# An attention, router and experts kernel: column-group logits for the last batch, held weight loads, choices as bits, four flag operations

## The chip, the cores and the metric

The kernel runs on one core of a Trainium2 chip, in one launch. The metric is the device time of that launch in microseconds. Five engines work at once and hand over by semaphores: TensorE (PE), VectorE (DVE), ScalarE (ACT), GpSimd (POOL) and SyncE (SP, which only issues DMA transfers here). Weight loads of TensorE are shown as PEld.

## What is computed

Windowed attention over 8 batches of 576 tokens with 8 heads of 64 gives a row x of 512 numbers for each of 4608 tokens. A router then assigns every token to one of 8 experts. It takes all 4608 x 8 logits from the largest down, and each expert takes at most 576 tokens. Each expert applies its two matrices to its tokens.

```python
# heads 0 to 3: the last 32 keys; heads 4 to 7: every 4th of the last 128
x = softmax(scale * q @ k.T, masked) @ v          # as 4608 rows of 512
logits = x @ w_gate                               # 4608 x 8
for idx in np.argsort(-logits.flatten()):
    tok, e = idx // 8, idx % 8
    if assigned[tok] >= 0 or counts[e] >= 576: continue
    assigned[tok] = e; counts[e] += 1
for e in range(8):
    mask = assigned == e
    out[mask] = np.maximum(x[mask] @ w1[e], 0) @ w2[e]
```

## The kernel before

The program lists its operations with the engine, a cost, what each depends on and a boost. A list scheduler (`Schedule`) in the program puts them in one order, and every engine executes its own in that order. So a changed cost or boost moves operations on all engines, even where the code beside it stays as it is. An engine stands still at an operation whose inputs are not there, and what is behind it on that engine waits too.

**Attention** runs batch by batch. `tokens()` (L652) computes the router's logits for the last batch alone (`DIRECT` = 7): in four groups, one for each 128 of the 512 features (`g`), it uses a tile of x as weights and 8 columns of the gate matrix as the moving side (L664). Copies (L674 on VectorE, L272 on ScalarE) bring the logits from PSUM to `Lt`, 36 chunks of 128 tokens with 8 logits. Earlier batches go another way: the gate matrix is the weights, in column groups (L597), and the logits come back through L605 and L618.

**The router** (class `Router`) works on `Lt`. `choose()` (L892) finds each token's best open expert (`M`), a sortable key and a one-hot row `oh0`. Where an expert has more than 576 candidates, a search over the keys finds its threshold. In the first round this is `search_alone()` (L835): coarse counts, then steps of flags and counts. VectorE writes the flags `G` for 36 chunks in `PARTS` = 5, 15 and 16 chunks of 16 columns (L792, L790), TensorE counts them with one matmul a chunk (L857), and VectorE and TensorE turn the counts into the next step's base (L870, L871). The later rounds' searches (`search`, `counts` L778) run beside the experts before them. `expert()` (L969) takes the largest full expert from `em`, and its index `eidx` (L976) is what SP reads to address the weights. `members()` marks its tokens (`pr` L983, `te` L985, `ge` L987); slots and a list `idx` of 576 tokens follow.

**The experts.** In each of 8 rounds `gather()` (L1242) fetches the 576 rows of x by five indirect DMAs on POOL (L1249, tiles `xg0` to `xg4`, from `xd` in DRAM), TensorE transposes them (L1263), ScalarE and VectorE split them into a high and a low part (`xh`, `xl`). GEMM1 is L1300, GEMM2 is L1342. `weights()` (L1140) loads `w1` and `w2` in 8 pieces each of 256 KB (`raw`, L1150, SP's queue), ScalarE makes the high part (`w1h`, `w2h`, L1137), and the low part comes from VectorE or, in the pairs of `ADDED`, from ScalarE and an accumulating DMA on POOL's queue (L1158, L1160). ScalarE also copies the output tiles `y` out of PSUM (L1137), and POOL scatters them (L1368). `behind()` (L1390) makes some loads of rounds 0 and 1 depend on the second gather:

```python
    def behind(r, f):
        return [got[r, 1]] if r < len(AHEAD_W) and f >= AHEAD_W[r] else []
```

Of the kernel before, what the change touches and what calls it, by code (L numbers as in the profile page):

```python
# [8 lines left out]
F32 = mybir.dt.float32  # L9
F32R = mybir.dt.float32r  # L10
BF = mybir.dt.bfloat16
I32 = mybir.dt.int32
U16 = mybir.dt.uint16
AF = mybir.ActivationFunctionType
OP = mybir.AluOpType
# [19 lines left out]
PARTS = (5, 15, 16)  # L35
# [4 lines left out]
RAW1, D_R, NQ, AHEAD_W = 8, 262, (2, 2), (3,)  # L40
# [19 lines left out]
def consts():  # L60
# [32 lines left out]
    f["pri"] = np.broadcast_to((NE - np.arange(NE))[None, :], (128, NE)).astype(np.float32)  # L93
# [149 lines left out]
def attention(tc, ctx, C, load_const, T, xd, Lt, R):  # L243
# [399 lines left out]
    def coarse(c0, c1, x, late):  # L643
        for c in range(c0, c1):
            g, used, use_ = PRE.take()
            f = op("DVE", 290, lambda c=c, g=g: R.coarse(c, g), [x, *used], late)
            counted[0] = op("PE", 60, lambda c=c, g=g: R.coarse_counts(c, g), [f, ready["c", 3], counted[0]], late)
            use_.append(counted[0])

    def tokens(un):  # L650

        b, u = un.b, un.u  # L652
        c0, c1 = b * S // 128, (b * S + S) // 128
        parts = [(c, 0, 128) for c in range(-(-b * S // 128), c1)]
        half = (c0, 64, 64) if b % 2 else (c1, 0, 64)
        late = B_K if b < B - 1 else B_E
        pt = Buf(PV)
        o = lambda c, p, n: pt.tile[p:p + n, NE * (c - c0):NE * (c - c0) + NE]

        def logits(gs):  # L660
            for c, p, n in parts + [half]:
                for g in gs:
                    t0 = 128 * c + p - b * S
                    nc.tensor.matmul(o(c, p, n), xt_[b, g // 2][0][:, g % 2, t0:t0 + n], wgp[:, g, :NE],  # L664
                                     start=(c == parts[0][0] and g == 0), stop=(g == 3), skip_group_check=True)

        t = un.op("PE", 1050, lambda: logits([0]), [*xt_[b][:3], ready["w"]], late, pt)
        t = un.op("PE", 1050, lambda: logits([1]), [t], late)
        t = un.op("PE", 1050, lambda: logits([2]), [t, *ch_[b]], late)
        t = un.op("PE", 1050, lambda: logits([3]), [t, *xt_[b]], late)  # L670
        for kk in range(2):
            xt_[b, kk][2].append(t)
        ca = parts[0][0]
        xs_ = [un.op("DVE", 200, lambda: nc.vector.tensor_copy(  # L674
            Lt[:, ca:c1], pt.tile[:, NE * (ca - c0):NE * (c1 - c0)].rearrange("p (c e) -> p c e", e=NE)), [t], late),
            un.op("ACT", 250, lambda: act(Lt[half[1]:half[1] + 64, half[0]], o(*half)), [t], late)]
        pt.users += xs_
        if b < B - 1:
            hl_.append(xs_[1])
        x = un.op("DVE", 1000, lambda: R.choose(c0, c1), [*xs_, *(hl_ if b == B - 1 else ())], late)  # L680
        coarse(c0, c1, x, B_P if b < B - 1 else late - u * P_U)
# [55 lines left out]
class Router:  # L737


    def __init__(self, tc, ctx, C, Lt):  # L740
        nc = tc.nc
        self.tc, self.C = tc, C
        self.pf = ctx.enter_context(tc.tile_pool(name="r_fix", bufs=1))
        self.Lt = Lt
        self.A = self.pf.tile([128, NCH], F32, name="A")
        self.PR = self.pf.tile([128, 32], F32, name="PR")
        self.M = self.pf.tile([128, NCH], F32, name="M")
        self.V0 = self.pf.tile([128, NCH], F32, name="V0")
# [148 lines left out]

    def copies(self, oh, eng):
# [70 lines left out]
    def expert(self, em):  # L969

        nc, pw = self.tc.nc, self.pw
        self.ohe = pw.tile([128, NE], F32, name="ohe")
# [3 lines left out]
        nc.vector.tensor_scalar(self.eidx, em[:1], -1.0, float(NE), op0=OP.mult, op1=OP.add)  # L976

    def members(self):

        nc, pw = self.tc.nc, self.pw  # L980
        ohe, gg = self.ohe, self.gg
        oe = pw.tile([128, NCH, NE], F32, name="pr", bufs=1)
        nc.vector.tensor_tensor(oe, self.oh, ohe[:, None, :].to_broadcast([128, NCH, NE]), op=OP.mult)  # L983
        te = pw.tile([128, NCH], F32, name="te")
        nc.vector.tensor_reduce(te, oe, axis=AX.X, op=OP.add)  # L985
        ge = self.ge = pw.tile([128, 2, NCH], BF, name="ge")
# [120 lines left out]
def moe(tc, ctx, C, R, xd, w1, w2, out):  # L1107
# [31 lines left out]
    E, gemm1_end, x_users, got = {}, {}, {}, {}  # L1139

    def weights(n, r, f, deps):

        raw, old, use = RAW[n].take()

# [97 lines left out]
    def gather(r, ix, box):  # L1242

        done = []
        for m, n in enumerate(MSZ):
# [6 lines left out]
            g = op("POOL", 1040, get, [ix, *old], B_G, lat=T_G if r else 2600)  # L1252
# [130 lines left out]
    def round_(r):  # L1383
# [6 lines left out]
        W[r] = [weights("1", r, f, [en, *behind(r, f)]) for f in range(NF)]  # L1390

    def behind(r, f):

        return [got[r, 1]] if r < len(AHEAD_W) and f >= AHEAD_W[r] else []

    round_(0)
    for r in range(NE):
        W2 = [weights("2", r, f, [EN[r], *behind(r, NF)]) for f in range(NF)]
# [81 lines left out]
```

## Time and profile before

| | us |
|---|---|
| three runs | 713.92, 715.23, 717.02 (median 715.23) |
| the profiled execution | 717.54 |
| its span, first to last instruction | 715.8 |
| PE busy | 673.1 (94%) |
| VectorE busy | 485.2 (68%) |
| ScalarE busy | 292.0 (41%) |
| POOL busy | 137.7 (19%) |
| mean granted TensorE clock | 0.962 |

The span divides into attention (to 212), the first round's search (212 to 229), its listing and gather (229 to 245), then expert 0 (245 to 310) and the other seven. A granted clock of 1.00 is TensorE's upper level, 0.50 its lower. Idle time of an engine costs only where the chain of waits passes through it; that chain is followed back from the last instruction.

### The profile page before, as it was taken

To read this page: it belongs to the slowest core of one execution; us is meant where nothing else is said; L and a number is where in the kernel's file an instruction comes from. 1 tells how busy PE (TensorE), PEld (TensorE's weight loads), DVE (VectorE), ACT (ScalarE), POOL (GpSimd) and SP (SyncE) were. 2 spreads that over 40 slices of the span, in tenths; PEclk is the share of its full clock that TensorE was granted. 3 is DMA by queue.
4 is the path that set the end of the run, shared out by engine and by line. 5 is a ranking of instruction groups with operands and counts; after the bars stand their busy time and mean duration, and the time that the engine had idled before them with its cause. 6 is when DMAs were issued, how large, how long until landed. Compare 5 with 4: busy or idle time off the path is not lost.

```text
span 715.8 us, 17384 instructions
## 1 busy us (share of the span) xinstructions
PE 673.1 (94%) x6577; PEld 590.1 (82%) x6579; DVE 485.2 (68%) x2085; ACT 292.0 (41%) x616; POOL 137.7 (19%) x204
## 2 busy tenths in 40 slices
PE   7899999999974799799999999999999999999995
PEld 5788899989973598689889779879978978988984
DVE  5467867778447789589679878968877964823300
ACT  3345554553520483576234423523523534424310
POOL 6111111100000332641410310310311131221011
PEclk9899999999975799999999999999999999999998
DMA  9999999982210674987323513602621384123001
GB/s 251 267 252 263 277 321 234 281 225 56 68 35 33 212 155 112 286 184 222 97 67 119 170 63 91 217 31 56 227 87 53 124 286 143 50 70 97 1 22 44
DMA packets 58524, 104.60 MB, mean 146 GB/s; under 512 B 6212, under 2 KB 27844, under 8 KB 58436
## 3 DMA queue, kind: packets, MB, share of 16 engines
q1 hardware_dynamic: 49096, 78.32, 38.5%
q0 software_dynamic: 9344, 25.17, 12.8%
q8 instruction: 51, 0.84, 0.5%
q14 instruction: 33, 0.27, 0.1%
HBM read 78.31 MB, written 18.87 MB: 136 GB/s over the span
## 4 chain that ended last, share of the span: by engine, by line
PE 73%; issue 12%; DVE 6%; DMA 4%; POOL 3%; ACT 1%; SPq 0%; POOLq 0%; DVEq 0%
PE ph L1300 24%; PE py L1342 15%; PE pS L506 9%; PE px L514 6%; PE pS L503 3%; PE px L564 3%; DMA xg<-xd,idx 2%; PE pm L486 2%; PE pz L778 2%; PE ptx L1263 2%; PE py L1345 1%; POOL out L1368 1%; PE py L1347 1%; DMA qs<-in_qd 1%; PE px L597 1%
## 5 line engine op out<-in xcount | busy, mean ns | idle before, releaser
L1342 PE MATMUL py<-w2h,hb 128*128 128x512 f32 x512 | 172.5, 401 | 1.3 <-issue 1.3
L1300 PE MATMUL ph<-xh,w1h 128*128 128x256 f32 (+1 forms) x512 | 138.7, 301 | 0.0
L1300 PE MATMUL ph<-xl,w1h 128*128 128x256 f32 (+1 forms) x512 | 136.2, 296 | 0.0
L1300 PE MATMUL ph<-xh,w1l 128*128 128x256 f32 (+1 forms) x512 | 136.0, 296 | 0.0
L1342 PEld LDWEIGHTS py<-w2h,hb 128*128 128x128 f32 x512 | 96.7, 189 | 21.5 <-issue 2.4
L1137 ACT ACTIVATE hb<-ph 128x256 fp32r<-128x256 f32 (+2 forms) x192 | 59.8, 346 | 103.9 <-PE ph L1300 103.5
L1342 PE MATMUL py<-w2l,hb 128*128 128x512 f32 x256 | 100.9, 394 | 0.7 <-DVE w2l L1138 0.5
L1300 PEld LDWEIGHTS ph<-xh,w1h 128*128 128x128 f32 x512 | 91.5, 189 | 0.6 <-ACT xh L1137 0.2
L1300 PEld LDWEIGHTS ph<-xh,w1l 128*128 128x128 f32 x512 | 91.6, 190 | 0.0
L1300 PEld LDWEIGHTS ph<-xl,w1h 128*128 128x128 f32 x512 | 91.5, 190 | 0.0
L506 PE MATMUL pS<-q,k 128*80 128x96 f32 (+1 forms) x672 | 83.7, 266 | 0.0
L1368 POOL DMA_INDIRECT out<-y,idx x40 | 40.1, 1003 | 203.6 <-ACT y L1137 142.8
L1320 DVE SCALAR_TENSOR_TENSOR hb<-ph,hb 128x320 fp32r<-128x320 f32 (+1 forms) x128 | 57.4, 453 | 29.7 <-ACT hb L1137 26.8
L456 ACT ACTIVATE E<-pS 96x384 f32<-96x384 f32 (+1 forms) x96 | 46.8, 487 | 74.9 <-PE pS L506 73.3
L506 PEld LDWEIGHTS pS<-q,k 128*80 128x80 f32 (+1 forms) x672 | 69.2, 160 | 0.3 <-issue 0.3
L1137 ACT ACTIVATE y<-py 128x512 f32<-128x512 f32 (+1 forms) x40 | 23.9, 597 | 103.4 <-PE py L1342 90.8
L493 DVE CUSTOM_DVE_ANT_0 junkm<-pm,const 128x80 bf16<-128x80 f32 (+1 forms) x336 | 59.7, 243 | 7.8 <-PE pm L486 7.5
L1342 PEld LDWEIGHTS py<-w2l,hb 128*128 128x128 f32 x256 | 48.5, 190 | 10.3 <-DVE w2l L1138 1.1
L514 PE MATMUL px<-v,E 81*64 81x65 f32 (+1 forms) x1344 | 48.3, 225 | 4.4 <-ACT E L456 2.5
L514 PEld LDWEIGHTS px<-v,E 81*64 81x64 f32 (+1 forms) x1344 | 43.1, 138 | 9.2 <-issue 2.9
L1137 ACT ACTIVATE w1h<-raw 128x512 fp32r<-128x512 f32 x64 | 38.5, 628 | 29.2 <-DMA raw<-in_moe_w 28.8
L1249 POOL DMA_INDIRECT xg<-xd,idx x40 | 40.3, 1007 | 50.1 <-PE ph L1300 31.1
(171 smaller groups left out, 1019.1 us busy)
## 6 DMA issues: line engine op xcount, KB each, us to landing
raw<-in_moe_w SPq DMA_DIRECT2D x128, 256.0 KB, 4.4
v<-in_vp SPq DMA_DIRECT2D x8, 780.0 KB
v<-in_vd SPq DMA_DIRECT2D x8, 650.0 KB
xd<-xs SPq DMA_DIRECT2D x16, 288.0 KB, 6.8
xd<-xs SPq DMA_DIRECT2D x32, 144.0 KB, 10.6
w2l<-raw POOLq DMA_DIRECT2D x16, 256.0 KB
qs<-in_qp SPq DMA_DIRECT2D x7, 576.0 KB, 9.2
k<-in_kp SPq DMA_DIRECT2D x7, 576.0 KB, 10.4
```

The source lines that it names most:

```text
L456: e = self.op("ACT", 380, lambda j=j, pS=pS: nc.scalar.activation(self.E[:self.nk, j * self.gs:j * self.gs + self.gs], pS.tile[:, :self.gs ...
L493: nc.vector.tensor_tensor_reduce(out=jk[:, c - c0, :nk], in0=pm[:, (c - c0) * nk:(c - c0 + 1) * nk], in1=mm[:, min(1, (c if self.kind == 0 ...
L503: nc.tensor.matmul(pS[:nk, c - c0], ls[:64 + n, c], self.r[:64 + n, :2 * nq], start=(c == c0), stop=False, skip_group_check=True)
L506: nc.tensor.matmul(pS[:nk, c - c0], self.Ks[c], self.Qm[c], start=False, stop=True, skip_group_check=True)
L514: nc.tensor.matmul(px[64 * a:64 * a + 64, c - c0], lh, self.V[c][a], start=True, stop=True)
L564: nc.tensor.transpose(t[:, c], src, C["identf"])
L1137: act = lambda o, i, f=AF.Copy: nc.scalar.activation(o, i, f)
L1249: nc.gpsimd.indirect_dma_start(out=xg[:n], out_offset=None, in_=xd, in_offset=bass.IndirectOffsetOnAxis(ap=box[0][:n, m:m + 1], axis=0))
L1300: nc.tensor.matmul(o, a[:, d * 128:d * 128 + 128], b[:, d, c0:c1], start=((d, i) == pairs[0]), stop=((d, i) == pairs[-1]))
L1320: hl = op("DVE", 335 if j == 0 else 400, lambda: nc.vector.scalar_tensor_tensor(hb[:, CAP + c0:CAP + c1], o, 0.0, hb[:, c0:c1], op0=OP.max ...
L1342: nc.tensor.matmul(py, x, w, start=(f + i == 0), stop=(f == NF - 1 and i == 2))
L1368: s = nc.gpsimd.indirect_dma_start(out=out, out_offset=bass.IndirectOffsetOnAxis(ap=box[0][:n, m:m + 1], axis=0), in_=y[:n], in_offset=None)
```

## The change

It has five parts.

1. `PARTS` becomes 3, 8, 12 and 13: the lone search's flags are written in four operations.
2. `tokens()` turns the last batch's logits round: the gate matrix (32 columns, 24 of them zero) is the weights, in four column groups for four chunks of 128 tokens, and a fifth matmul does the half chunk. VectorE copies the 128x192 result to SBUF, TensorE transposes it in two matmuls, and copies bring it to `Lt`. The costs and boosts that the scheduler is told change with it.
3. `bits()`: two VectorE operations for each batch make a number with bit e set for each best expert e. The priority `pri` becomes a power of two, `eidx` is read from its exponent in two operations, and in round 0 `members()` multiplies, masks one bit and compares, on 36 columns in place of 288.
4. `behind()` goes. In rounds 0 and 1 POOL writes one number of the tile `raw` of the first held piece (f = 3, f = 4) behind the second gather in the planner's dependences, and the loads from that piece on, those of w2 too, depend on it.
5. The planner's cost of a gather is 1250 in place of 1040, the latency in round 0 is 2500 in place of 2600.

The core of the diff:

```diff
-PARTS = (5, 15, 16)
+PARTS = (3, 8, 12, 13)
-RAW1, D_R, NQ, AHEAD_W = 8, 262, (2, 2), (3,)
+RAW1, D_R, NQ, AHEAD_W = 8, 262, (2, 2), (3, 4)
...
-    f["pri"] = np.broadcast_to((NE - np.arange(NE))[None, :], (128, NE)).astype(np.float32)
+    f["pri"] = np.broadcast_to(2.0 ** (NE - 1 - np.arange(NE))[None, :], (128, NE)).astype(np.float32)
+    f["bit"] = np.broadcast_to(2.0 ** np.arange(NE)[None, :], (128, NE)).astype(np.float32)
...
+        op("DVE", 350, lambda: R.bits(c0, c1), [x, ready["c", 3]], late - 2000)
...
     def tokens(un):
         b, u = un.b, un.u
-        c0, c1 = b * S // 128, (b * S + S) // 128
-        parts = [(c, 0, 128) for c in range(-(-b * S // 128), c1)]
-        half = (c0, 64, 64) if b % 2 else (c1, 0, 64)
+        c0, c1 = -(-b * S // 128), (b * S + S) // 128
+        t0 = 128 * c0 - b * S
         late = B_K if b < B - 1 else B_E
-        pt = Buf(PV)
-        o = lambda c, p, n: pt.tile[p:p + n, NE * (c - c0):NE * (c - c0) + NE]
-        def logits(gs):
-            for c, p, n in parts + [half]:
-                for g in gs:
-                    t0 = 128 * c + p - b * S
-                    nc.tensor.matmul(o(c, p, n), xt_[b, g // 2][0][:, g % 2, t0:t0 + n], wgp[:, g, :NE],
-                                     start=(c == parts[0][0] and g == 0), stop=(g == 3), skip_group_check=True)
-        t = un.op("PE", 1050, lambda: logits([0]), [*xt_[b][:3], ready["w"]], late, pt)
-        t = un.op("PE", 1050, lambda: logits([1]), [t], late)
-        t = un.op("PE", 1050, lambda: logits([2]), [t, *ch_[b]], late)
-        t = un.op("PE", 1050, lambda: logits([3]), [t, *xt_[b]], late)
+        pt, pg = Buf(PV), Buf(PV)
+        lg = L4.tiles[0][:, (b % 2) * S:]
+        def logits(g):
+            x = xt_[b, g // 2][0][:, g % 2]
+            for k in range(c1 - c0):
+                nc.tensor.matmul(pt.tile[32 * k:32 * k + 32, :128], wgp[:, g], x[:, t0 + 128 * k:t0 + 128 * k + 128],
+                                 start=(g == 0), stop=(g == 3), skip_group_check=True)
+            nc.tensor.matmul(pt.tile[:32, 128:128 + t0], wgp[:, g], x[:, :t0], start=False, stop=(g == 3), skip_group_check=True)
+        t = un.op("PE", 330, lambda: logits(0), [*xt_[b][:3], ready["w"]], late, pt)
+        t = un.op("PE", 330, lambda: logits(1), [t], late)
+        t = un.op("PE", 330, lambda: logits(2), [t, *ch_[b]], late)
+        t = un.op("PE", 330, lambda: logits(3), [t, *xt_[b]], late)
         for kk in range(2):
             xt_[b, kk][2].append(t)
-        ca = parts[0][0]
+        k = un.op("DVE", 330, lambda: nc.vector.tensor_copy(lg[:, :128 + t0], pt.tile[:, :128 + t0]), [t, *L4_["free"]], late)
+        pt.users.append(k)
+        def gates():
+            nc.tensor.transpose(pg.tile[:, :128], lg[:, :128], C["identf"])
+            nc.tensor.matmul(pg.tile[128 - t0:, 128:160], lg[:32, 128:128 + t0], C["identf"][:32, :32], start=True, stop=True)
+        t = un.op("PE", 180, gates, [k], late, pg)
         xs_ = [un.op("DVE", 200, lambda: nc.vector.tensor_copy(
-            Lt[:, ca:c1], pt.tile[:, NE * (ca - c0):NE * (c1 - c0)].rearrange("p (c e) -> p c e", e=NE)), [t], late),
-            un.op("ACT", 250, lambda: act(Lt[half[1]:half[1] + 64, half[0]], o(*half)), [t], late)]
-        pt.users += xs_
-        if b < B - 1:
-            hl_.append(xs_[1])
-        x = un.op("DVE", 1000, lambda: R.choose(c0, c1), [*xs_, *(hl_ if b == B - 1 else ())], late)
-        coarse(c0, c1, x, B_P if b < B - 1 else late - u * P_U)
+            Lt[:, c0:c1], pg.tile[:, :128].rearrange("p (c e) -> p c e", e=32)[:, :, :NE]), [t], late),
+            un.op("ACT", 250, lambda: act(Lt[128 - t0:, c0 - 1], pg.tile[128 - t0:, 128:128 + NE]), [t], late)]
+        pg.users += xs_
+        x = un.op("DVE", 1000, lambda: R.choose(c0 - 1, c1), [*xs_, *hl_], late)
+        coarse(c0 - 1, c1, x, late - u * P_U)
...
+    def bits(self, c0, c1):
+        nc = self.tc.nc
+        t = self.pf.tile([128, 8, NE], F32, name="bits", bufs=2)[:, :c1 - c0]
+        nc.vector.tensor_tensor(t, self.oh0[:, c0:c1], self.C["bit"][:, None, :].to_broadcast([128, c1 - c0, NE]), op=OP.mult)
+        nc.vector.tensor_reduce(self.bits0[:, c0:c1], t, axis=AX.X, op=OP.add)
...
-        nc.vector.tensor_scalar(self.eidx, em[:1], -1.0, float(NE), op0=OP.mult, op1=OP.add)
+        nc.vector.tensor_scalar(self.eidx, em[:1].bitcast(I32), 23, None, op0=OP.arith_shift_right)
+        nc.vector.tensor_scalar(self.eidx, self.eidx, -1.0, 126.0 + NE, op0=OP.mult, op1=OP.add)
...
+        if self.oh is self.oh0:
+            ti = pw.tile([128, NCH], I32, name="ti")
+            nc.vector.tensor_scalar(ti, self.bits0, self.em, None, op0=OP.mult)
+            nc.vector.tensor_scalar(ti, ti, 2 ** (NE - 1), None, op0=OP.bitwise_and)
+            nc.vector.scalar_tensor_tensor(ge, ti[:, None, :].to_broadcast([128, 2, NCH]), 1.0, gg, op0=OP.is_ge, op1=OP.mult)
+            return
...
+        if n == "1" and r < len(AHEAD_W) and f == AHEAD_W[r]:
+            gate[r] = op("POOL", 100, lambda: nc.gpsimd.memset(raw[:1, :1], 0.0), [got[r, 1], *old], B_G)
+        if r in gate:
+            deps = [*deps, gate[r]]
...
-            g = op("POOL", 1040, get, [ix, *old], B_G, lat=T_G if r else 2600)
+            g = op("POOL", 1250, get, [ix, *old], B_G, lat=T_G if r else 2500)
...
-        W[r] = [weights("1", r, f, [en, *behind(r, f)]) for f in range(NF)]
+        W[r] = [weights("1", r, f, [en]) for f in range(NF)]
...
-        W2 = [weights("2", r, f, [EN[r], *behind(r, NF)]) for f in range(NF)]
+        W2 = [weights("2", r, f, [EN[r]]) for f in range(NF)]
```

The order of attention's work changes on all engines from the fourth batch on. Three places follow. A row is line, operation, written tile, read tiles, columns, and what it waits for by semaphore; numbers behind a name tell buffers apart.

TensorE at the end of attention (`xs` are rows of x that L564 transposes, `xt` the transposed tiles, `L` the copied logits, `pre` the coarse flags). Before:

```order
L564 MATMUL px_138<-const_63,xs_122 128x128 [waits DVE_49]
L564 MATMUL px_138<-const_63,xs_122 128x128 x2
L564 MATMUL px_140<-const_63,xs_122 128x128 [waits DVE_49]
L564 MATMUL px_140<-const_63,xs_122 128x128 x2
L664 MATMUL px_139<-wgp,xt_126 128x8 [waits DVE_49,Activation_49]
L664 MATMUL px_139<-wgp,xt_126 128x8 x3
L664 MATMUL px_139<-wgp,xt_126 64x8
L770 LDWEIGHTS pre_129 [waits DVE_49]
L770 MATMUL pz<-oh_75,pre_129 128x8
```

and with the change:

```order
L664 MATMUL px_139<-xt_125,wgp 32x128 [waits Activation_49]
L664 MATMUL px_139<-xt_125,wgp 32x128 x3
L666 MATMUL px_139<-xt_125,wgp 32x64
L664 MATMUL px_139<-xt_125,wgp 32x128 x4
L666 MATMUL px_139<-xt_125,wgp 32x64
L664 MATMUL px_139<-xt_127,wgp 32x128 x4
L666 MATMUL px_139<-xt_127,wgp 32x64
L664 MATMUL px_139<-xt_127,wgp 32x128 [waits DVE_49,Activation_49]
L664 MATMUL px_139<-xt_127,wgp 32x128 x3
L666 MATMUL px_139<-xt_127,wgp 32x64
L678 MATMUL px_141<-const_63,L_128 128x128 [waits DVE_49]
L679 MATMUL px_141<-const_63,L_128 64x32
```

The first three groups stood among the attention matmuls further up; now all four stand behind the last transposes, and a transpose follows them.

POOL in round 1 (`out` is a scatter, `w1l` an accumulating load). Before:

```order
L1367 MEMSET spacer 1x1 [waits Pool_49]
L1368 DMA out<-y_3269,idx 4608x512 [waits DMASW1_49,Activation_49]
L1249 DMA xg_3252<-xd,idx 128x512 [waits DMASW2_49,DVE_49]
L1249 DMA xg_3253<-xd,idx 128x512 [waits DMASW3_49]
L1249 DMA xg_3254<-xd,idx 128x512 [waits DMASW4_49]
L1249 DMA xg_3255<-xd,idx 128x512 [waits DMASW5_49]
L1249 DMA xg_3256<-xd,idx 64x512 [waits DMASW6_49]
L1160 DMA w1l_3239<-raw_3211 128x512 [waits DMASW7_49,DMAHW3_49,PE_49,Activation_49]
L1160 DMA w1l_3240<-raw_3212 128x512 [waits DMASW0_49,DMAHW4_49,PE_49,Activation_49]
```

and with the change:

```order
L1394 MEMSET spacer 1x1 [waits Pool_49]
L1395 DMA out<-y_3297,idx 4608x512 [waits DMASW1_49,Activation_49]
L1276 DMA xg_3280<-xd,idx 128x512 [waits DMASW2_49,DVE_49]
L1276 DMA xg_3281<-xd,idx 128x512 [waits DMASW3_49]
L1276 DMA xg_3282<-xd,idx 128x512 [waits DMASW4_49]
L1276 DMA xg_3283<-xd,idx 128x512 [waits DMASW5_49]
L1276 DMA xg_3284<-xd,idx 64x512 [waits DMASW6_49]
L1168 MEMSET raw_3240 1x1
L1187 DMA w1l_3267<-raw_3239 128x512 [waits DMASW7_49,DMAHW3_49,PE_49,Activation_49]
L1394 MEMSET spacer 1x1 [waits Pool_49]
L1395 DMA out<-y_3298,idx 4608x512 [waits DMASW0_49,Activation_49]
L1187 DMA w1l_3268<-raw_3240 128x512 [waits DMASW1_49,PE_49,DMAHW4_49,Activation_49,Pool_49]
```

The memset on the first held tile stands behind all five gathers, as it does in round 0, and scatters come between the accumulations that follow. SP's load of that tile waits for POOL; before, no load did, since the dependence on the second gather was one of the planner only and gave no wait.

ScalarE in round 1 (`ohr` are the copies for the counts, `xh` the high part of the gathered rows). Before:

```order
L1137 ACTIVATE w1h_3223<-raw_3211 128x512 [waits DMAHW3_49]
L1158 ACTIVATE w1l_3239<-w1h_3223 128x512 [waits Activation_49]
L1137 ACTIVATE w1h_3224<-raw_3212 128x512 [waits DMAHW4_49]
L1158 ACTIVATE w1l_3240<-w1h_3224 128x512 [waits Activation_49]
L1137 ACTIVATE w1h_3225<-raw_3213 128x512 [waits DMAHW5_49]
L902 ACTIVATE ohr<-oh 128x1152 [waits DVE_49]
L1158 ACTIVATE w1l_3241<-w1h_3225 128x512 [waits Activation_49]
L1137 ACTIVATE w1h_3226<-raw_3214 128x512 [waits DMAHW0_49]
L1158 ACTIVATE w1l_3242<-w1h_3226 128x512 [waits Activation_49]
L1137 ACTIVATE y_3270<-py_3205 128x512 [waits PE_49]
L1137 ACTIVATE w1h_3227<-raw_3215 128x512 [waits DMAHW3_49]
L1158 ACTIVATE w1l_3243<-w1h_3227 128x512 [waits Activation_49]
```

and with the change:

```order
L1159 ACTIVATE w1h_3251<-raw_3239 128x512 [waits DMAHW3_49]
L1185 ACTIVATE w1l_3267<-w1h_3251 128x512 [waits Activation_49]
L916 ACTIVATE ohr<-oh 128x1152 [waits DVE_49]
L1159 ACTIVATE y_3298<-py_3233 128x512 [waits PE_49]
L1159 ACTIVATE xh<-ptx_3235 128x4x128 [waits PE_49]
L1159 ACTIVATE xh<-ptx_3235 128x4x128 [waits DVE_49,PE_49]
L1159 ACTIVATE w1h_3252<-raw_3240 128x512 [waits DMAHW4_49,Pool_49]
L1159 ACTIVATE y_3296<-py_3234 128x512 [waits DMASW5_49,PE_49]
L1185 ACTIVATE w1l_3268<-w1h_3252 128x512 [waits Activation_49]
L1159 ACTIVATE w1h_3253<-raw_3241 128x512 [waits DMAHW5_49]
```

Before, the high parts of all eight pieces of `w1` stood ahead of the first `xh`, which is the next row; now the first of them (`raw_3240`, the held one) stands behind two `xh` and ahead of one `y`.

## Rows read from the trace of the kernel before

**Rows 1.** Stages (start:end, us, busy and count by engine, PEclk, DMA share, GB/s).

```profile
190.00:212.00 22.00, 19.03 (x265) 17.33 (x262) 8.35 (x34) 7.56 (x15) 0.00 (x0) 0.89 0.24 55
...
294.00:299.00 5.00, 1.00 (x6) 0.54 (x5) 0.46 (x2) 0.46 (x1) 3.51 (x5) 1.00 1.06 372
299.00:303.00 4.00, 4.00 (x24) 3.31 (x22) 2.47 (x10) 1.29 (x3) 3.10 (x6) 0.57 1.12 207
303.00:704.00 401.00, 397.65 (x2737) 349.67 (x2736) 273.77 (x867) 159.61 (x360) 81.17 (x116) 1.00 0.36 112
```

**Rows 2.** Chain of waits, end of attention (start us, us, engine, tile, line, count).

```profile
195.93 0.73 PE px L597 x12
196.66 0.48 PE px L564 x3
...
198.87 1.00 PE px L664 x10
...
207.20 0.67 DVE xt L575
...
208.01 2.17 PE px L664 x10
```

**Rows 3.** Chain of waits, one step of the lone search.

```profile
213.49 0.70 DVE G L792 x2
...
214.24 0.96 PE pz L857 x31
```

**Rows 4.** Waits of TensorE, 190 to 312 us (total us, times, longest).

```profile
PE py L871 <- DVE flaga L870: 1.5, 6, 0.3
```

**Rows 5.** VectorE's groups by shape, 212 to 230 us (busy us, mean ns | idle before).

```profile
L792 DVE SCALAR_TENSOR_TENSOR G<-V,py,kb 128x256 bf16<-128x256 f32 x2 | 1.0, 484 | 0.0
...
L792 DVE SCALAR_TENSOR_TENSOR G<-V,py,kb 128x80 bf16<-128x80 f32 x2 | 0.6, 306 | 0.5 <-PE py L871 0.5
...
L985 DVE TENSOR_REDUCE te<-pr 128x36 f32<-128x288 f32 x1 | 0.5, 453 | 0.0
...
L983 DVE TENSOR_TENSOR pr<-oh,ohe 128x288 f32<-128x288 bf16 x1 | 0.4, 439 | 0.0
...
L940 DVE TENSOR_SCALAR gg<-V,found 128x36 bf16<-128x36 f32 x1 | 0.2, 225 | 0.0
...
L976 DVE TENSOR_SCALAR eidx<-em 1x1 int32<-1x1 f32 x1 | 0.1, 134 | 0.0
```

**Rows 6.** Chain of waits, the first gathers of rounds 0 and 1.

```profile
237.33 5.59 DMA xg<-xd,idx
...
289.25 9.47 DMA xg<-xd,idx
```

**Rows 7.** Timeline of TensorE at the two gathers [idle before <-releaser].

```profile
244.97 0.74 PE L1300 MATMUL ph<-xh,w1h 128*128 128x256 f32 x4
...
247.03 0.46 PE L1263 MATMUL py<-const,xg 64*128 64x64 f32 x4
...
298.76 0.66 PE L1263 MATMUL ptx<-const,xg 128*128 128x128 f32 x4 [4.00 <-DMA xg<-xd,idx]
```

**Rows 8.** Timeline of POOL at the two gathers.

```profile
242.87 0.91 POOL L1249 DMA_INDIRECT xg<-xd,idx  x1 [0.30 <-issue]
...
284.11 0.88 POOL L1160 DMA_DIRECT2D w1l<-raw  x1
...
294.38 0.92 POOL L1249 DMA_INDIRECT xg<-xd,idx  x1 [0.30 <-issue]
```

**Rows 9.** Timeline of SP's DMA issues in round 1.

```profile
279.55 7.47 SPq L1150 DMA_DIRECT2D raw<-in_moe_w  x12
```

**Rows 10.** Timeline of ScalarE at the two gathers.

```profile
248.16 0.64 ACT L1137 ACTIVATE w1h<-raw 128x512 fp32r<-128x512 f32 x1
...
298.55 0.63 ACT L1137 ACTIVATE w1h<-raw 128x512 fp32r<-128x512 f32 x1 [4.68 <-DMA raw<-in_moe_w]
```

**Rows 11.** DMA issues on the page (KB each, median us to landing).

```profile
raw<-in_moe_w SPq DMA_DIRECT2D x128, 256.0 KB, 4.4
```

More of the change, by code (lines that the diff above doesn't have):

```diff
@@ L749, in __init__ @@
         self.oh0 = self.pf.tile([128, NCH, NE], BF, name="oh0")
+        self.bits0 = self.pf.tile([128, NCH], F32, name="bits0")
         self.key0 = self.pf.tile([128, NCH], I32, name="key0")
@@ L971, in expert @@
         nc, pw = self.tc.nc, self.pw
+        self.em = em
         self.ohe = pw.tile([128, NE], F32, name="ohe")
@@ L981, in members @@
         ohe, gg = self.ohe, self.gg
+        te = pw.tile([128, NCH], F32, name="te")
+        ge = self.ge = pw.tile([128, 2, NCH], BF, name="ge")
+        if self.oh is self.oh0:
[4 more added lines that the diff above has]
+            return
         oe = pw.tile([128, NCH, NE], F32, name="pr", bufs=1)
         nc.vector.tensor_tensor(oe, self.oh, ohe[:, None, :].to_broadcast([128, NCH, NE]), op=OP.mult)
-        te = pw.tile([128, NCH], F32, name="te")
         nc.vector.tensor_reduce(te, oe, axis=AX.X, op=OP.add)
-        ge = self.ge = pw.tile([128, 2, NCH], BF, name="ge")
         nc.vector.tensor_tensor(ge, te[:, None, :].to_broadcast([128, 2, NCH]), gg, op=OP.mult)
@@ L1138, in moe @@
     sub = lambda e, o, a, b: e.tensor_tensor(o, a, b, op=OP.subtract)
-    E, gemm1_end, x_users, got = {}, {}, {}, {}
+    E, gemm1_end, x_users, got, gate = {}, {}, {}, {}, {}
     def weights(n, r, f, deps):
         raw, old, use = RAW[n].take()
+        if n == "1" and r < len(AHEAD_W) and f == AHEAD_W[r]:
+            gate[r] = op("POOL", 100, lambda: nc.gpsimd.memset(raw[:1, :1], 0.0), [got[r, 1], *old], B_G)
+        if r in gate:
+            deps = [*deps, gate[r]]
         def load():
@@ L1389, in round_ @@
         X[r] = gather(r, ix, BOX[r])
-        W[r] = [weights("1", r, f, [en, *behind(r, f)]) for f in range(NF)]
-    def behind(r, f):
-        return [got[r, 1]] if r < len(AHEAD_W) and f >= AHEAD_W[r] else []
+        W[r] = [weights("1", r, f, [en]) for f in range(NF)]
     round_(0)
     for r in range(NE):
-        W2 = [weights("2", r, f, [EN[r], *behind(r, NF)]) for f in range(NF)]
+        W2 = [weights("2", r, f, [EN[r]]) for f in range(NF)]
         expert(r, X[r], BOX[r], W[r], W2)
```

## Prediction

> **What bounds the kernel now.** I read the stages first. TensorE is busy for 397.65 of the 401 us from 303 on [rows 1], so there only TensorE work counts, and whatever is gained ahead of it is kept: everything behind moves up by as much. The idle time lies before: 3.0 us of the 22 at the end of attention, and 4.0 of the 5 between 294 and 299 [rows 1]. The next 4.00 us run at a granted clock of 0.57, so between the two levels 1.2 and 2.4 GHz, after that idle stretch; at the full level they would have needed 4.00 x 0.57 = 2.28, so the pause costs another 1.72. Then I read the chain that ended last. It passes through the last logits [rows 2], six steps of the lone search [rows 3, 4], the first gather with 5.59 us and the second gather with 9.47 us [rows 6]. These are the places that the change touches. The second gather is the largest: TensorE waits 4.00 us for it [rows 7].
>
> The sum is made against the profiled execution (717.54 us). It is 2.31 above the median of the runs shown (715.23), so I subtract the sum from the median.
>
> **The last logits.** Removed are 40 small matmuls in four groups of about 1 us on the chain, of which one stands in the rows (198.87, 1.00), and the last, 2.17 at 208.01 [rows 2]. Added are 20 matmuls in column groups. The nearest row is L597, 12 such matmuls with 288 columns in 0.73, or 0.06 each [rows 2]; five with 128 columns or fewer are 0.3 at most. The first three groups now stand behind the last transposes, where TensorE waits for the 0.67 copy anyway [rows 2], so they cost about 0.2 in all. Behind the last group come new links on the chain: a VectorE copy of 128x192 (the one of 288 columns stands with 0.67 on the chain [rows 2], I take 0.5), two transposes (four take 0.66 [rows 7], so 0.33), and two handovers of about 0.05 each, the width of the gaps between the chain's rows. So 2.17 becomes 0.3 + 0.5 + 0.33 + 0.1 = 1.23, a gain of 0.94. The three earlier groups free 3.0 us of TensorE time ahead of 206. TensorE is the busiest engine there (19.03 of 22, VectorE 8.35 [rows 1]), but ScalarE's exponentials and VectorE's divisions have to follow, so I take a third of it, 1.0. Together **-1.9**, with -3.9 as one end (all 3.0 kept) and 0 as the other (the added handovers cost three times as much and attention, whose order on all engines changes from the fourth batch on, loses a little).
>
> The row shows no gap at a change of tile: L597 ends at 195.93 + 0.73 = 196.66 [rows 2] and the next tile's matmuls start at that very time. The Trainium skill's "TensorEngine Tiling (Array Packing)", section Key Properties, says that a change of tiling mode drains TensorE, which speaks against column groups squeezed between other work. With a drain as long as one of the transposes (0.17, an estimate) for two changes the sum would be 0.3 less of a gain; by the row it is nothing.
>
> **Flags in four operations.** One step is 0.70 for the first two flag operations and 0.96 for the 31 matmuls behind them [rows 3]. An operation on 256 elements takes 484 ns, one on 80 takes 306 [rows 5]: 1.01 ns an element, 225 fixed, of which the overlap with the next leaves about 0.15 (0.70 for two, the second of 469 to 484, leaves 0.22 to 0.23 for the first with 80 elements). A fourth operation therefore ends the flags 0.15 later; the last piece shrinks from 16 to 13 matmuls of 0.031 (0.96 / 31), which gives back 0.09. That is +0.06 a step, six steps [rows 4]: **+0.35**, against the aim. The ends are 0 and +0.6 (0.1 a step, if the handover is dearer).
>
> **First choices as bits.** Two operations of 36 elements (225 ns each, L940) replace two of 288 (439 and 453 ns, L983 and L985); the third stays as long. Minus 0.44 on a VectorE that sets this stretch. The expert's index takes a second, dependent operation, 134 ns (L976) [rows 5]. **-0.3** in round 0. In the later rounds only the 0.13 remains, hidden behind TensorE. The two new operations for each batch lie beside attention, where VectorE has room (8.35 of 22 even at its end [rows 1]); the last batch's pair stands behind the flags of its coarse counts, while TensorE still counts. Nothing for them; were the cover gone it would be 0.4.
>
> **Weight loads behind the gather, round 0.** Before, SP ran on with all loads and the gathers had to share. The gather of the first 128 rows took 5.59 [rows 6]. The least contended one here, the last, is issued at 242.87 [rows 8] and read at 247.03 [rows 7]: 4.16 at most. With 4.2 the first would be there 1.4 earlier. The moved count group, which needs ScalarE's copies first, and the spacing of the gathers (1.25 from one to the next) eat some: the first GEMM needs the third gather and starts at 244.97 [rows 7]. I take **-0.9**; ends -2.0 and +1.0. What the gate adds: the memset stands behind all five gathers on POOL, so SP's load for w1h3 starts no earlier than 242.87 + 0.91 = 243.78 [rows 8]. At the median landing of 4.4 [rows 11] it is there at 248.2; ScalarE wants it at 248.16 [rows 10]. There is no slack, but no loss either.
>
> **The same, round 1.** Twelve loads were issued from 279.55 on over 7.47 us [rows 9], ahead of the gather at 289.25. Now four go ahead; the other loads wait. Between the ends 4.2 (as in round 0's last gather) and 9.47 (as now), I take 5.0, since the transfers on POOL's own queue, three accumulations from 284.11 on [rows 8], remain. 289.25 + 5.0 = 294.25, and TensorE begins to wait at 298.76 - 4.00 = 294.76 [rows 7]. The wait goes, and with it the slow clock: -5.7. What is late next is ScalarE. It executes in order, and its w1h4 now comes from the first gated load: 294.38 + 0.92 = 295.30 [rows 8], plus 4.4, is 299.7. Before, ScalarE stood at a load until 298.55 [rows 10] and TensorE did not wait for it; now the copy of a finished output tile, which frees a PSUM bank for GEMM2, is queued behind. 1.2 us later I charge with 0.9. **-4.8**; ends -5.7 and -1.5.
>
> Sum: -1.9 + 0.35 - 0.3 - 0.9 - 4.8 = -7.55. 717.54 becomes 710.0; from the median 715.23 it is 707.7.
>
> **Rivals.** *POOL's own queue keeps the gather late.* The accumulations and two scatters stand ahead of it there and are not gated. With 8.5 in place of 9.47 TensorE still waits 289.25 + 8.5 - 294.76 = 3.0 and its clock still falls: round 1 gives 1.0, and the total is -1.9 + 0.35 - 0.3 - 0.9 - 1.0 = -3.75, so 711.5. For it: the memory traffic of 294 to 299 is at a share above 1 [rows 1] after SP's issues ended at 287.0. Against it: twelve loads outweigh three accumulations. The Trainium skill's "DMA: Bandwidth & Descriptors", section Issuing engines are not separate DMA queues, says that transfers of all issuers run on the same 16 engines and interleave. By that rule both the held loads and the accumulations count, and the time lies between this rival's and the forecast.
>
> *The gated loads are late: slower.* The load that ScalarE waited for until 298.55 [rows 10] had been issued by 279.55 + 7.47 = 287.0 [rows 9], so some loads need 11.5, not 4.4. If the gated ones do, w1h3 comes at 255.3, 7.1 after ScalarE wants it, and w1h4 at 306.8, 8.3 after 298.55. The copies that free PSUM stand behind both, and TensorE waits about 6 and 7, with 1.7 of slow clock after each: -7.55 + 0.9 + 16.4 = +9.75, so 725.0. It decides from a landing of some 8 us on. Against it: the gathers are nearly through when these loads start, so they have the engines to themselves.
>
> *Attention's new order opens gaps.* The planner now sees cheaper logits and places work of the last five batches differently. TensorE has only 3.0 us of idle time in the last 22 [rows 1]; a gap of 1 us in each of the five batches would be +5 and leave -2.55, so 712.7.
>
> **How the numbers follow.** Forecast 0.70, POOL's queue 0.14, late loads 0.07, attention 0.09. The forecast's own ends, all favourable, are -3.9 + 0 - 0.3 - 2.0 - 5.7 = -11.9 (703.3); the attention case sets the upper end. Range 703.5 to 712.8. Half a per cent, 3.6 us, is about what can be told from no change: faster is below 711.65. That is the forecast nearly whole (0.68), two thirds of the POOL case (0.09) and a little of the attention case (0.02): 0.79 faster. Late loads are slower in full: 0.07. The rest, 0.14, is the same.
>
> **What would show it.** Right: no idle row of TensorE at the second gather's first transposes and a clock of 1.00 from 294 to 303; the first GEMM starting 2 to 4 us earlier than 244.97; last logits of 0.3 with a copy and two transposes behind; a search step's two rows adding up to 1.7 where 0.70 + 0.96 stand; ScalarE's idle time before w1h4 at 1 us or so. Wrong: a first gather in round 1 above 6 us, TensorE waiting for ScalarE in either GEMM, or an attention that ends later than 206.

## The result, and the profile after

The changed kernel takes 0.9889 of the time before, with a 95% interval of 0.9841 to 0.9937: medians of 710.91 us (705.34 to 713.28, 7 runs) and 717.02 us (713.92 to 721.55, 7 runs). The ratio is one of means; of 717.02 it is 8.0 us less, between 4.5 and 11.4, and the two medians differ by 6.1. The forecast was 7.55 less, which from the median known then, 715.23, made 707.7. The profiled execution took 705.34, the shortest of its seven, and that of before 717.54, so the two traces differ by more (a span of 703.5 against 715.8) than the kernels do.

The stages of the changed kernel, in the columns of [rows 1]:

```profile
190.00:212.00 22.00, 16.83 (x314) 14.33 (x312) 12.88 (x60) 5.22 (x11) 0.00 (x0) 0.88 0.21 51
290.00:300.00 10.00, 6.95 (x50) 5.02 (x48) 7.79 (x33) 5.65 (x11) 2.49 (x5) 1.00 0.91 279
300.00:692.00 392.00, 390.15 (x2691) 346.05 (x2690) 268.39 (x849) 159.18 (x359) 83.27 (x118) 1.00 0.37 115
```

The last batch's logits and what follows them up to the first operation that needs all logits (`M`), in the chain of waits:

```profile
199.60 0.91 PE px L565 x6
200.51 0.40 PE px L664 x8
...
202.09 0.37 DVE L L674
...
202.51 0.33 PE px L678
...
203.60 0.21 DVE M L886
...
205.51 0.12 DVE bits L909
...
206.15 0.19 DVE junkc L850 x2
```

The same place before, in the timeline of TensorE, with `M` from the chain and the stage from 208 to 209:

```profile
205.59 0.55 PE L564 MATMUL px<-const,xs 128*128 128x128 f32 x3
206.61 0.55 PE L564 MATMUL px<-const,xs 128*128 128x128 f32 x3 [0.47 <-DVE xs L526]
208.01 2.16 PE L664 MATMUL px<-wgp,xt 128*128 128x8 f32 x10 [0.85 <-DVE xt L575]
```

```profile
210.63 0.21 DVE M L879
```

```profile
208.00:209.00 1.00, 0.99 (x5) 1.00 (x6) 0.00 (x0) 0.00 (x0) 0.00 (x0) 0.50 0.90 235
```

From the first of the last six transposes to `M` it is 203.60 - 199.60 = 4.00 now and 210.63 - 205.59 = 5.04 before. The old last group, 2.17 in [rows 2], ran at the lower clock level, 0.50. The kernel e1 below has the same order on TensorE and VectorE there, and in its profile the group ran at the upper level:

```profile
202.00 1.24 PE L664 MATMUL px<-wgp,xt 128*128 128x8 f32 x10 [0.84 <-DVE xt L575]
```

```profile
202.00:203.00 1.00, 1.00 (x9) 0.98 (x9) 0.00 (x0) 0.00 (x0) 0.00 (x0) 1.00 0.88 233
```

There it took 1.24, and 4.12 from the six transposes to `M`. So from these transposes on the new form gains 1.0 against the profile of before and 0.1 against the old form at the upper level. The group became four groups in a row, 1.5 us up to 202.0, the copy of 0.37 and two transposes up to 203.1. What else was gained lies ahead of the transposes.

One step of the lone search, against [rows 3]:

```profile
208.91 0.28 DVE G L799
...
209.24 0.22 PE pz L864 x3
...
209.51 1.18 PE pz L864 x33
```

The first piece is three chunks, so TensorE starts early, but then the flags of the last piece set the step: 0.28 + 0.22 + 1.18 and three handovers. The six steps from the first count to the last take 13.11 us in place of 12.81.

The gathers, TensorE against [rows 7] and POOL against [rows 8]:

```profile
234.39 0.66 PE L1290 MATMUL py<-const,xg 128*128 128x128 f32 x4
...
237.67 0.72 PE L1327 MATMUL ph<-xh,w1h 128*128 128x256 f32 x4
```

```profile
230.50 1.46 POOL L1276 DMA_INDIRECT xg<-xd,idx  x1 [3.36 <-DVE idx L1124]
...
281.98 1.04 POOL L1276 DMA_INDIRECT xg<-xd,idx  x1 [0.31 <-DVE A L1071]
...
287.10 0.92 POOL L1276 DMA_INDIRECT xg<-xd,idx  x1 [0.30 <-issue]
288.01 0.09 POOL L1168 MEMSET raw<- 1x1 f32 x1
```

The first GEMM starts at 237.67, not 244.97; half of these 7.3 us lies at the start of attention and is spread between executions, as e6 shows. In round 1 the memset opens the gate at 288.01. The wait of 4.00 us for the gathered rows is gone, and the clock stays at its upper level, 1.00, from 290 on. But there is a new wait. These are TensorE, VectorE and ScalarE there:

```profile
287.39 0.46 PE L785 MATMUL pz<-G,ohr 128*128 128x64 bf16 x9
287.68 0.63 PE L1290 MATMUL ptx<-const,xg 128*128 128x128 f32 x4
...
292.96 0.45 PE L785 MATMUL pz<-G,ohr 128*128 128x64 bf16 x9 [2.56 <-DVE G L799]
```

```profile
286.17 0.82 DVE L799 SCALAR_TENSOR_TENSOR G<-V,delta,const 128x576 bf16<-128x576 f32 x1
...
290.82 0.32 DVE L822 STREAM_TRANSPOSE Q<-pz 128x128 f32<-128x128 f32 x1 [3.68 <-remote]
...
292.09 0.82 DVE L799 SCALAR_TENSOR_TENSOR G<-V,delta,kb 128x576 bf16<-128x576 f32 x1
```

```profile
290.88 0.60 ACT L1159 ACTIVATE xh<-ptx 128x512 fp32r<-128x512 f32 x1 [4.74 <-remote]
...
295.09 0.62 ACT L1159 ACTIVATE w1h<-raw 128x512 fp32r<-128x512 f32 x1
```

TensorE ends the count group (L785) and the transposes (L1290) by 288.3, and goes on with GEMM2. VectorE, which needs the counts, starts at 290.82, and ScalarE, which needs the transposes, at 290.88, both after 3.7 to 4.7 us of idle time that the profile puts down to nothing it knows ("remote"). TensorE then waits 2.56 for the next flags. I call this the hold. ScalarE's w1h4, the first piece behind the gate, follows at 295.09 without waiting for its load. These are the landings of the loads issued from 284 to 294:

```profile
raw<-in_moe_w SPq DMA_DIRECT2D x8, 256.0 KB, 4.3
```

But ScalarE was itself held. In the kernels e9 and e10 below, which lack the hold, it waits 2.63 and 3.62 for this load, and in e10 the wait reaches TensorE through `xh` and `xl`:

```profile
296.42 0.63 ACT L1161 ACTIVATE w1h<-raw 128x512 fp32r<-128x512 f32 x1 [3.62 <-DMA raw<-in_moe_w]
```

```profile
299.09 0.69 DVE L1162 TENSOR_TENSOR xl<-ptx,xh 128x512 fp32r<-128x512 f32 x1 [1.27 <-ACT xh L1161]
```

```profile
299.84 0.66 PE L1292 MATMUL ptx<-const,xg 128*128 128x128 f32 x4 [1.51 <-DVE xl L1162]
```

### The profile page after: what moved, and what is told of

It is laid out like the page before. It is cut to its first block, busy times and chain, and to the rows that moved or that the text cites. A ratio compares the mean times of both kernels' runs of the same rounds, so it can differ in the third digit from the quotient of the medians.

```text
span 703.5 us, 17418 instructions
## 1 busy us (share of the span) xinstructions
PE 665.6 (95%) x6579; PEld 584.1 (83%) x6581; DVE 488.5 (69%) x2116; ACT 292.3 (42%) x616; POOL 138.2 (20%) x206
## 4 chain that ended last, share of the span: by engine, by line
PE 69%; DVE 12%; issue 12%; POOL 3%; DMA 2%; ACT 1%; another core or an unknown queue 1%; SPq 0%; POOLq 0%; DVEq 0%
PE py L1369 18%; PE ph L1327 17%; PE pS L507 9%; PE px L515 6%; PE pS L504 2%; PE px L565 2%; PE pm L487 2%; PE ptx L1290 2%; PE pz L785 2%; DVE hb L1347 1%; PE py L1372 1%; PE py L1374 1%; DMA qs<-in_qd 1%; POOL out L1395 1%; PE pz L864 1%
## 5 line engine op out<-in xcount | busy, mean ns | idle before, releaser
L507 PE MATMUL pS<-q,k 128*80 128x96 f32 (+1 forms) x672 | 82.9, 264 | 0.0
L507 PEld LDWEIGHTS pS<-q,k 128*80 128x80 f32 (+1 forms) x672 | 68.4, 158 | 0.0
```

The lines of the kernel that those rows point to most:

```text
L507: nc.tensor.matmul(pS[:nk, c - c0], self.Ks[c], self.Qm[c], start=False, stop=True, skip_group_check=True)
```

## The experiments

The times of two executions of one kernel lie up to 10 us apart, so the runs are read by stages. The columns of this table come from one trace each: from the start of the 401st of the 672 score matmuls (L506, L507 after) to the search's first count (tail), the search, from its last count to the first GEMM (listing), from there to the first GEMM of round 1 (expert 0), and from there to the end (rest). The last column is the ratio to before with its interval, where a kernel was timed more than once; e9, e10 and e11 took 704.25, 706.49 and 711.16 once, beside 720.48 of before.

| kernel | tail | search | listing | expert 0 | rest | ratio |
|---|---|---|---|---|---|---|
| before | 86.81 | 12.81 | 18.31 | 65.39 | 405.4 | 1 |
| e1_gate_only | 85.89 | 12.81 | 17.91 | 62.57 | 404.3 | 0.992 (0.989 to 0.995) |
| e3_logits_only | 82.92 | 12.82 | 18.94 | 67.12 | 404.7 | 0.993 (0.989 to 0.997) |
| e2_no_gate | 83.57 | 13.11 | 18.70 | 67.50 | 401.8 | 0.993 (0.990 to 0.996) |
| e7_gate_r1 | 83.58 | 13.12 | 19.96 | 64.88 | 402.6 | 0.992 (0.989 to 0.995) |
| e8_old_planner | 83.59 | 13.11 | 17.64 | 61.82 | 407.9 | 0.991 (0.987 to 0.994) |
| changed | 83.57 | 13.11 | 17.53 | 63.68 | 402.2 | 0.989 (0.984 to 0.994) |
| e6_again | 83.59 | 13.11 | 17.42 | 63.73 | 402.7 | 0.987 (0.984 to 0.991) |
| e4_old_logits | 87.56 | 13.12 | 17.46 | 61.48 | 402.5 | 0.988 (0.983 to 0.993) |
| e11, the same again | 87.37 | 13.12 | 17.46 | 61.33 | 404.3 | |
| e5_best | 83.41 | 12.58 | 17.52 | 63.83 | 403.7 | 0.989 (0.985 to 0.994) |
| e9_shift16 | 83.60 | 13.10 | 17.40 | 61.15 | 403.9 | |
| e10_shift48 | 84.42 | 13.11 | 17.48 | 62.52 | 404.4 | |

Two theories stood against each other first: the forecast's (A), by which the gathers give most, and one by which the end of attention does (B).

**e1_gate_only.** The kernel before, with the gate's four lines in `weights()`, `AHEAD_W` = (3, 4) and without `behind()`:

```diff
+        if n == "1" and r < len(AHEAD_W) and f == AHEAD_W[r]:
+            gate[r] = op("POOL", 100, lambda: nc.gpsimd.memset(raw[:1, :1], 0.0), [got[r, 1], *old], B_G)
+        if r in gate:
+            deps = [*deps, gate[r]]
```

> The kernel before with the held loads alone (part 4; planner's gather cost as before). Theory A, the forecast's: the two gathers are most of the gain, so 5 to 6 us less than before; in the trace TensorE's wait at the second gather falls from 4.0 to under 1 us, and the 3.4 us at half clock behind it go. Theory B: the accumulations and scatters on POOL's own queue keep the second gather late, and the gain of the change is at the end of attention; then 1 to 3 us less, with a wait of 2 to 3 us left there.

It was 5.7 less (3.7 to 7.8), the number of A. The rival of POOL's own queue falls: three accumulations still stood ahead of the gather, and TensorE's waits around the second gather no longer name it. By the columns the gate gives 3.2 of this, 0.40 in the listing and 2.82 in expert 0, where TensorE now waits 1.7 for VectorE's `xl` behind ScalarE's late load, as in e10. The 0.92 of the tail is the clock of the last logits, and the 1.1 of the rest is not explained.

**e2_no_gate.** The changed kernel with the old dependence:

```diff
-        if r in gate:
-            deps = [*deps, gate[r]]
...
+        W[r] = [weights("1", r, f, [en, *behind(r, f)]) for f in range(NF)]
```

> The changed kernel without the held loads (the dependence of the planner alone, as before). A: 1 to 3 us less than before, TensorE waits about 4 us for the second gather again. B: 4 to 6 us less than before, nearly as fast as the changed kernel.

It was 711.29, 5.2 less than before (3.2 to 7.2), so here B's number came. But the wait is back as A says:

```profile
PE ptx L1285 <- DMA xg<-xd,idx: 3.6, 1, 3.6
```

Expert 0 rises from 63.7 to 67.5 and the listing from 17.5 to 18.7. Both theories hold in part: the wait at the gather is what A says, and there is a gain elsewhere that A lacks. It is in the columns tail and rest.

**e3_logits_only.** The kernel before with the new `tokens()` alone (the diff ahead of the prediction).

> The kernel before with the last batch's logits in column groups alone (part 2). A: about 1.9 us less than before, the lone search's first flags 1 to 4 us earlier. B: 4 to 6 us less, and the search's first flags as much earlier.

5.1 less (2.5 to 7.6), the number of B; A's 1.9 lies outside. The tail is 82.92 against 86.81 of before and 85.89 of e1, which differ by the clock of the old last group: 3.0 less at one level, 3.9 with the slow group. In listing and expert 0 this trace loses 2.4 of it again.

**e4_old_logits.** The changed kernel with the old `tokens()`, **e11** the same again.

> The changed kernel with the old last logits (40 small matmuls). A: 5 to 6.5 us less than before, so about 2 us more than the changed kernel. B: 2 to 4 us less than before.

The tail is 87.56 and 87.37, 3.8 to 4.0 more than in the changed kernel, with the last group at the lower clock again (2.16 and 1.99). Yet the median is 708.48, 8.6 less than before (5.0 to 12.2): B's 2 to 4 less falls, and A's 5 to 6.5 can stand. By whole times it can't be told from the changed kernel, so part 2's worth is read from the tail alone. Its expert 0 is 2.2 shorter: the hold isn't there, though the order of every engine behind attention is the changed kernel's.

**e7_gate_r1.** The changed kernel with `AHEAD_W` = (8, 4), so that round 0 holds nothing.

> The changed kernel with the loads held in round 1 alone. Theory A: holding them in round 0 is worth about 1 us; from the search's end to the first GEMM 18.5 us in place of 17.5, the first gather waiting about 2 us for its data again, and round 1 as in the changed kernel. Rival: the first gather is limited by its own latency and the count group moved behind it, then 17.5 stays.

The listing is 19.96, and the wait for the first gather is there again:

```profile
PE py L1290 <- DMA xg<-xd,idx: 2.1, 1, 2.1
```

The gate of round 0 is worth 2.4 beside e7, 1.2 beside e2 and, with the rest of the kernel as before, 0.4 (e1); A had said about 1. The rival falls.

**e8_old_planner.** The changed kernel with 1040 and 2600 for a gather.

> The changed kernel with the planner's old cost of a gather (1040, 2600). Theory E: the 2 us that rounds 2 to 7 are shorter in the changed kernel (402.2 from the first GEMM of round 1 to the end, 405.4 before) come from this part's order; then 404 to 405 again. Theory F: they come from the other parts or are idle moments of single executions; then about 402.

The rest is 407.9, more than either theory says and 5.2 to 5.7 more than the changed kernel's 402.2 and 402.7. Of the 5.7, 3.4 lie in round 1, with a stretch at a lower clock that no other trace has there:

```profile
333.00:337.00 4.00, 4.00 (x14) 3.31 (x13) 3.68 (x15) 1.78 (x4) 1.08 (x1) 0.57 0.13 50
```

The other 2 lie in rounds 2 to 5. These four rounds take 229.0 to 230.0 in all nine traces with the new cost, and 231.4 (e8), 231.9 (e3) and 232.6 (before) with the old one. But e1, which has the old cost and there the order of before on TensorE and VectorE, takes 229.5. So a gain of 2 to 3 us by the planner's cost, which I gave no term, is likely, and not shown: single executions differ by as much.

**e6_again.** The changed kernel, for a second profile.

> The changed kernel itself, once more, for a second profile. If the 2.6 us that TensorE waited for the search's flags at the second gather belong to the kernel, they are there again, with the same place in the order; if they were of that execution alone, the stretch from the first GEMM of round 0 to that of round 1 is some 2 us shorter than its 63.7. The clock dips ahead of 60 us should differ from profile to profile, in number too. Time as the changed kernel's, 6 to 9 us less than before.

The hold is there again (expert 0 63.73, TensorE's 2.6 us for the flags), so it belongs to the kernel. The profiles of e5 and e7, whose TensorE order is the same, have it too, with 2.67 and 2.64. The spread of the times does not belong to it: ahead of the 401st score matmul it took 127.2 us here and 123.5 in the first profile, 127.0 in that of before and 121.0 in that of e1, whose attention is the same as before's. The stages 20 to 30 and 40 to 60 us of before, of the changed kernel and of e6:

```profile
20.00:30.00 10.00, 9.69 (x131) 8.97 (x132) 4.91 (x33) 2.77 (x6) 1.98 (x3) 0.68 1.08 279
40.00:60.00 20.00, 18.45 (x294) 17.03 (x294) 12.80 (x100) 8.60 (x17) 1.99 (x3) 0.91 1.06 249
```

```profile
20.00:30.00 10.00, 8.86 (x132) 8.14 (x133) 5.64 (x35) 3.65 (x7) 1.98 (x3) 0.83 1.07 278
40.00:60.00 20.00, 19.37 (x349) 18.00 (x347) 15.24 (x113) 9.04 (x18) 1.99 (x3) 1.00 1.06 265
```

```profile
20.00:30.00 10.00, 10.00 (x135) 9.28 (x134) 4.50 (x32) 2.63 (x5) 1.99 (x3) 0.69 1.07 276
40.00:60.00 20.00, 17.21 (x318) 15.95 (x314) 13.54 (x103) 8.40 (x17) 1.99 (x3) 1.00 1.07 257
```

The clock (the column behind POOL) falls at up to two places in the first 65 us, at others from profile to profile (here below 1.00 in both stages of before, in the first alone of the others), while the transfers are at a share above 1.

**e9_shift16** and **e10_shift48.** The changed kernel with tiny fill matmuls behind the first ones, while TensorE waits for the first loads:

```diff
     keep_clock(nc, warm, fill, F0)
+    for _ in range(16):
+        nc.tensor.matmul(fill[:, :16], warm[:, :128], warm[:, :16], start=True, stop=True)
```

> The changed kernel with 16 tiny fill matmuls (16 columns) more at TensorE's start, while it waits for the first loads: every later TensorE instruction stands 32 places further back, nothing else moves. Theory G: the 3 us by which TensorE's signals of the count group and the first transposes of round 1 are late hang on where these instructions stand in TensorE's instruction stream; then the hold goes or moves to another place, and from the first GEMM of round 0 to that of round 1 it takes 61 to 62 us. Theory H: the hold comes with the order and timing at the second gather; then it is there again and the stretch stays at 63.7.

> The same with 48 tiny matmuls, 96 places. G: 61 to 62 us in that stretch, or a hold at another place than in the changed kernel. H: 63.7 again, VectorE and ScalarE starting 3 us after the count group.

> The changed kernel with the old last logits, a second profile. Its first had no hold (61.5 us from GEMM1 of round 0 to that of round 1), with the same order on all engines behind attention as the changed kernel. If the hold is the kernel's own, 61.5 again; if it comes and goes from one execution to another, it may show 63.7.

With 16 the hold is gone, expert 0 is 61.15, VectorE starts behind the same count group after an ordinary wait:

```profile
287.73 0.32 DVE L824 STREAM_TRANSPOSE Q<-pz 128x128 f32<-128x128 f32 x1 [0.88 <-PE pz L787]
```

With 48 the hold is gone too: VectorE starts after the same ordinary wait of 0.88, at 288.36. Expert 0 is 62.52 for another reason, the 1.51 that TensorE waits behind ScalarE's late load. The rest is 1.7 and 2.2 longer, most of it in round 1 (60.6 and 61.1 between its first GEMM and the next round's, 58.7 in the changed kernel), where TensorE waits 1.2 and 2.4 for VectorE's `ge` in place of 0.4. So of what is gained without the hold, most (e9) or more than all (e10) is lost again there. In e4 and e11, one kernel, that round took 58.9 and 60.4, so this differs between executions.

G is borne out in its first half, that the hold goes; e4 and e11, which by the records have 4 TensorE instructions fewer ahead, lack it as well. But e9, e10 and e11 ran on another chip than e5, e6 and e7, which show it, and no profile of the changed kernel is on record from there. So that the place in TensorE's instruction stream decides whether the hold comes is likely, and not shown. What holds TensorE's signals back was not found.

**e5_best.** The changed kernel with three pieces again, the largest in the middle, and the last batch's bits inside the search's first step:

```diff
-PARTS = (3, 8, 12, 13)
+PARTS = (8, 16, 12)
-        op("DVE", 350, lambda: R.bits(c0, c1), [x, ready["c", 3]], late - 2000)
+        if c1 < NCH:
+            op("DVE", 350, lambda: R.bits(c0, c1), [x, ready["c", 3]], late - 2000)
...
+            if base is None and not last:
+                self.bits((B - 1) * S // 128, NCH)
```

> The changed kernel with PARTS (8, 16, 12) and with the last batch's two bit operations moved from ahead of the lone search's first test into its first step, where VectorE waits for TensorE's counts. Theory C: a fourth flag operation costs its fixed 0.15 us, and the bit operations stand uncovered on the chain; then a search step is 2.10 us or less in the trace (2.22 in the changed kernel, 2.16 before), and from the last transposes to the search's end 0.8 to 1.3 us go. Theory D: TensorE's counting sets a step and the bits are covered; then a step stays at 2.16 to 2.22 and nothing goes. The time itself, 0 to 1.5 us less than the changed kernel, is within its spread in both.

```profile
215.06 0.77 DVE G L800 x2
...
215.88 0.86 PE pz L865 x28
...
217.18 0.79 DVE G L800 x2
```

A step is 2.12 (215.06 to the next one's 217.18), the search 12.58: 0.53 less than in the changed kernel and 0.23 less than before. And from the start of the last transpose to the search's first count it is 6.62 in place of 6.79, 0.17 less. Theory D falls; C has the direction, but its numbers (a step of 2.10 or less, 0.8 to 1.3 in all) are just missed with 2.12 and 0.70. The edit changed the pieces and the bits at once, so their shares are read from these stretches, not tested one by one. The whole ratio, 0.989, can't show 0.7 us.

## Why the prediction was right, and where its steps were not

The sum was right and the range held the time, but several steps were off and made up for each other, so the good sum is in part luck.

- **The last logits**, -1.9: the tail fell by 3.0 (e3 against e1) to 4.0 (changed against e4), near the end that I gave as -3.9. The step that failed is "I take a third of it". Up to the first of the last six transposes the tail takes 78.56 in before and in e1, 75.71 in e3, 79.09 in e4 and in e11, 76.15 in the changed kernel: 2.85 and 2.94 less with the new logits. So nearly all of the 3.0 of TensorE time freed there was passed on. The other half of the term, 0.94 on the last group, is 1.0 in the pair of profiles and 0.1 against e1. I had read 2.17 as the price of the old group, but it is the price at the lower clock level; at the upper one it is 1.24. And all four groups now follow the transposes on the chain; I had put three of them into the wait for the copy, but TensorE reaches them after all transposes. No gap stands between the column groups and the transposes ahead of them (199.60 + 0.91 = 200.51), so the drain at a change of tiling mode that the Trainium skill's "TensorEngine Tiling (Array Packing)", section Key Properties, names is in no row here.
- **Flags in four operations**, +0.35: measured +0.30, by the step that the forecast named, and e5 shows that three pieces of another split beat both.
- **First choices as bits**, -0.3 and nothing in attention: attention pays 0.65 for them (83.57 against e3's 82.92). The cover that I named is gone at the last batch, where VectorE's pair stands on the chain (205.51): from the start of the last transpose to the search's first count it is 6.56 in e3 and 6.79 in the changed kernel. The other 0.4 lies ahead of the last transposes (75.71 and 76.15; with the old logits 78.56 and 79.09), and where it arises was not tried. In round 0 VectorE's new operations take 0.34 us less: 224 and 183 ns for the bits and 135 and 142 for the index, in place of 439 and 453 and of 134.
- **Round 0's gather**, -0.9: the listing fell by 0.78 with the bits in it, and e1, e2 and e7 give 0.4 to 2.4 for the gate. The first rows were read 234.39 - 230.50 = 3.9 us after their gather began, where I reckoned with 4.2.
- **Round 1's gather**, -4.8: expert 0 fell by 1.7 in the pair of profiles, by 2.8 in e1, and by 3.9 to 4.2 in e4, e11 and e9, where neither the hold nor a long wait for `xl` stands. The wait and the slow clock went as forecast. The 0.9 that I charged for ScalarE, which stands behind its first gated load, is hidden by the hold in the changed kernel; where the hold is missing the wait is there, and TensorE feels 1.5 to 1.7 of it in e10 and e1, and at most 0.5 in e4, e9 and e11. What I did not foresee is the hold, of 2.56 and more.
- **What had no term**: rounds 1 to 7, the rest, 3.2 us less in the pair, 1 to 4 in the others with the new gather cost. I let the scheduler's reordering count for attention alone, and as a loss. As e1 and e8 leave it, how much of this is the order and how much the single execution stays open.

The spans differ by 12.24: 3.58 ahead of the 401st score matmul, which is spread, then 3.24 - 0.30 + 0.78 + 1.71 + 3.23 by the columns. Without the first it is 8.7, within the measured interval. Of the rivals, POOL's own queue fell with e1. The late loads fell too: the gated load was late for ScalarE by up to 4.2 us (e1), not by 8, and no kernel was slower than before. Attention's new order opened no gaps that cost what it freed.

## What to carry over

A load that nothing needs yet can be held back until a transfer on the critical path has been issued: here that removed a wait of 4 us and the slow clock behind it, and the held loads came late by at most 1.7 us for TensorE. A price read from a row of TensorE holds for the clock level of that row: the same ten matmuls took 2.16 and 1.24. When an engine that is busy all the time loses work in front of a hand-over, expect nearly all of it on the chain, and look separately at what the new form adds behind the hand-over. Where a planner orders the program, a changed cost is a part of the change and needs a term of its own.

## What the runs showed of the hardware

The signals of a TensorE group can reach the other engines 3 us after its recorded end (a modelled one): VectorE and ScalarE started at 290.82 and 290.88 on counts and transposes that ended by 287.9 and 288.3, and the trace has the updates of TensorE's semaphore at 290.79 and 290.85, none of them between 288.3 and then. So it was in all four profiles of this TensorE order (changed, e5, e6, e7), each time 0.4 to 0.5 us after the last GEMM2 matmul that TensorE had in hand, and not in the two with 32 and 96 instructions put in front; the cause is open.

Profiles with the same work up to there differ by 6 us in the first 125 (121.0 in e1 and 127.0 in before), two of one program by 3.7 (123.5 and 127.2), with short idle times of TensorE and stretches at its lower clock level that fall elsewhere in each execution. The Trainium skill's "DMA: Bandwidth & Descriptors", section Issuing engines are not separate DMA queues, says that all issuers' transfers share the 16 engines; e1 agrees, since holding SP's loads alone was enough for POOL's gather.
